# Two score banks more for the first four query blocks of a window-attention and MoE kernel

## The chip, the cores and the metric

The kernel runs as one program on one core of a Trainium2 chip. The metric is the device time of one execution in microseconds. The engines are TensorE (PE; its weight loads are PEld), VectorE (DVE), ScalarE (ACT), GpSimd (POOL) and SyncE (SP), which here only issues transfers. Each works through its own queue in order.

## What is computed

Window attention (batch 4, 8 heads, 576 positions, head size 64, a window of 64), a dense feed-forward layer of width 2048 with squared ReLU, and a top-1 mixture of 8 experts of width 1024, all in fp32:

```python
def reference(**kwargs):
    ...
    attn_out = _attn_ref(**attn_kwargs)          # softmax(mask(q k^T / 8)) v, 0 <= i - j < 64
    x = attn_out.transpose(0, 2, 1, 3).reshape(B * S, H * D)        # 2304 x 512
    x = _moe_ref(x=x, **moe_kwargs)              # h = max(x w_in, 0); (h * h) w_out
    return _moe2_ref(x=x, **moe2_kwargs)         # the best expert's max(x w1, 0) w2, times its gate
```

## The kernel before

The 2304 tokens go through attention and the dense layer in nine supertiles of 256 tokens. A supertile is four query blocks of 64 positions, all eight heads at once; block g of the first eight (two supertiles, NE = 8) is called g0 to g7 here. Behind them come g8 to g35, and at last the experts.

One block is a chain of eight stages (the tuple ATT): scores on PE (`att_scores`, L349: a mask matmul, then eight matmuls into one PSUM bank), the row maximum on DVE (L375) and its scaling on ACT (L378), four exps on ACT (L396), the division on GpSimd (L412), four transposes on PE (L418), a copy on ACT (L423), sixteen value matmuls on PE (L433), and a split of the result into a high part `xh` on ACT (L168) and a low part `xl` on DVE (L169). All matmuls of the dense layers take three products of such halves (L172 to L174).

PSUM has eight banks of 512 columns. The first eight blocks put their scores into two of them in turn, y0 and y1 (`ybanks[g % 2]`); y2 and y3 take the value products, a0 and a1 the transposes, h0 and h1 the hidden layer of the dense layer, which begins after the first four blocks.

Beside attention, the dense layer's weights are prepared, 16 chunks f0 to f15 of 128 hidden units. They arrive as 64-bit floats, 1 MB a chunk, two chunks deep in the buffers `stg`. A chunk takes an Abs on ACT (L189), four passes on DVE (L205, L206, L207, L210), two casts on ACT to the high half (L226) and two subtractions on GpSimd, some on DVE, to the low half (L228). The load of chunk f + 2 is issued when the passes of f are through (`conv_b`). Then the chunk's up-projection (`gemm1`) may run for a supertile, with ReLU (L462) and square (L469, L471, L478) behind it, and its down-projection (`gemm2`).

The order of the program is laid out by hand in slots, one for each pair of supertile and chunk. `chain(i, ATT, g, gaps)` (L893) puts a block's stages into slots from i on; the loop at L946 writes them out slot by slot, from slot -PRE on. Supertile 0 has slots 0 to 4 alone, then supertiles 1 and 0 alternate. A scheduler then reorders each engine's queue by its own estimate of the times, so a change of slots can also move instructions that it does not name.

Of the kernel before, what the change touches and what calls it, by code (L numbers as in the profile page):

```python
# [49 lines left out]
def kernel(  # L50
# [24 lines left out]
    QB = ST // W  # L75
# [79 lines left out]
    def psum(tag, bufs):  # L155
        return pr.tile([P, 512], F32, tag, bufs)

    ybanks = [pspool.tile([P, 512], F32, tag=f"y{i}", name=f"y{i}") for i in range(2 * TT)]
# [24 lines left out]
    def conv_a(f):  # L183
        i = (br.at["tmp"] + 1) % 4
        assert i % 2 == 0
        c = [br.tile([P, 512], I32, "tmp", 4) for _ in range(2)]
        whole = tmp2[i // 2].rearrange("p t n -> p (t n)")
        w = stg2[f % 2].bitcast(I32).rearrange("p t (n two) -> p (t n) two", two=2)
        nc.scalar.activation(whole.bitcast(F32), w[:, :, 1].bitcast(F32), ACTF.Abs)  # L189
        conv[f] = w[:, :, 0], w[:, :, 1], whole, c  # L190
# [109 lines left out]
    def load_q(g, n=1):  # L300
        b, i = divmod(g, NB)
        if g >= NE:
            qd[g] = br.tile([P, W, HP], F32, "qd", 1)
            nc.sync.dma_start(qd[g], qT[b, :, i])
            return
        qt = qfirst[:, g:g + n]
        for j in range(n):
            qk[g + j] = qfirst[:, g + j]
        if g > 1:
            for part in (qt[:D, :, W:], qt[D:, :, :W]):  # L310
                nc.scalar.copy(part, zero[:part.shape[0]].unsqueeze(2).unsqueeze(3).to_broadcast(part.shape))
        else:
            with tc.issue_after(made.ins):
                nc.vector.memset(qt[:D, :, W:], 0.0)
                nc.vector.memset(qt[D:, :, :W], 0.0)
        for half in range(2):
            rows = slice(half * D, half * D + D)
            nc.sync.dma_start(qt[rows, :, half * W:half * W + W, :], qT[b, rows, i:i + n])

    def lay_q(g):  # L320

        qk[g] = er.tile([P, HP, 2, W], F32, "q", 2)
        if g < NE + 2:
            with tc.issue_after(made.ins):
                nc.gpsimd.memset(qk[g][:D, :, 1, :], 0.0)
                nc.gpsimd.memset(qk[g][D:, :, 0, :], 0.0)
        d = qd.pop(g).rearrange("p s h -> p h s")
        for half in range(2):
            rows = slice(half * D, half * D + D)

            if g < NE + 5:
                nc.scalar.copy(qk[g][rows, :, half, :], d[rows])
            else:
                nc.gpsimd.tensor_copy(qk[g][rows, :, half, :], d[rows])  # L334
# [4 lines left out]
    def load_k(g, n=1):  # L339
        b, i = divmod(g, NB)  # L340
        nc.sync.dma_start(kfirst[:, g:g + n] if g < NB else kring[:, g % 4:g % 4 + n], kT[b, :, i:i + n])
# [7 lines left out]
    def att_scores(g):  # L349
        qt = qk.pop(g)  # L350
        k0 = g - 1 if g % NB else g
        if g < NE:
            ps = ybanks[g % 2]
            m = mask_b[:, 0 if g % NB else 1, :].unsqueeze(1).to_broadcast([P, HP, P])
            nc.tensor.matmul(ps.rearrange("p (h k) -> p h k", h=HP), lhsT=ident_b, rhs=m, start=True, stop=False)
        else:
            ps = psum("a", 2)
        for hp in range(HP):
            kt = kfirst[:, k0:k0 + 2] if g < NB else kring[:, k0 % 4:k0 % 4 + 2] if k0 % 4 < 3 else kring[:, 3::-3]
            nc.tensor.matmul(  # L360
                ps[:, hp * P:(hp + 1) * P], lhsT=qt[:, :, hp] if g < NE else qt[:, hp], rhs=kt[:, :, hp, :], start=g >= NE, stop=g >= NE or hp == HP - 1
            )
        if NE <= g < NS * QB - 1:
            lay_q(g + 1)
        if NE <= g < NS * QB - 2:
            load_q(g + 2)
        if NB < g < NS * QB - 3:
            load_k(g + 3)
        probs[g] = ps
# [510 lines left out]
    slot = {c: i for i, c in enumerate(order)}  # L880
    todo = {}
    ON_PE = (att_scores, att_transpose, att_values, gate_rank, early_pick, early_rows, early_tokens)

    def at(i, f, *args):
        todo.setdefault((i, f in ON_PE), []).append((f, args))

    def run(i, pe):
        for f, args in todo.pop((i, pe), ()):
            f(*args)
# [3 lines left out]
    def chain(i, stages, x, gaps, most=2):  # L893

        for f, gap in zip(stages, gaps):
            i += gap
            if f in ON_PE and i >= 0:
                while load.get(i, 0) >= most:
                    i += 1
                load[i] = load.get(i, 0) + 1  # L900
            at(i, f, x)
        return i

    ATT = (att_scores, att_max, att_exp, att_norm, att_transpose, att_evac, att_values, att_out)
    at(16, load_gates, 0)

# [2 lines left out]
            at(i + part, gate_dots, st, part)  # L909
        chain(i + E // 2, (gate_top, gate_rank, gate_slot), st, (0, 1, 1))  # L910

    PRE = 8
    for f in range(NF):
        i = max(-3, min(f - 1, slot[0, f] - 2))
        at(i, conv_c, f)
# [5 lines left out]
                  (0, load_k, 11), (0, load_k, 12), (0, load_wg, 0), (1, lay_q, NE), (1, load_q, NE + 1)):  # L921
        at(i, *l)
    for g in range(2 * QB):
        chain(g - PRE, ATT, g, (0, 1, 0, 1, 0, 1, 0, 1))
    for g in range(2 * QB, NS * QB):
        st, j = divmod(g, QB)
        i = slot[st, 0] - 19 + 4 * j
# [17 lines left out]
    conv_a(0)  # L945
    for i in range(-PRE, len(order) + LA):  # L946
        run(i, False)
# [207 lines left out]
```

## Time and profile before

| | |
|---|---|
| median of three runs | 835.53 us (834.1 to 836.63) |
| the profiled execution | 832.06 us, its span 829.9 us |
| PE busy | 787.3 us (95%) |
| DVE busy | 530.4 us (64%) |
| ACT busy | 398.8 us (48%) |
| POOL busy | 269.9 us (33%) |
| granted PE clock, mean | 0.987 of full speed |

The busy shares are means over stages with different limits: the opening, in which the first blocks and the dense layer's weights are prepared, the dense layer, and the experts behind it. The opening has to be read by stretches. A wait in these tables is idle time of an engine, with the instruction that ended it.

### The profile page before, as it was taken

To read this page: it belongs to the slowest core of one execution; us is meant where nothing else is said; L and a number is where in the kernel's file an instruction comes from. 1 tells how busy PE (TensorE), PEld (TensorE's weight loads), DVE (VectorE), ACT (ScalarE), POOL (GpSimd) and SP (SyncE) were. 2 spreads that over 40 slices of the span, in tenths; PEclk is the share of its full clock that TensorE was granted. 3 is DMA by queue.
4 is the path that set the end of the run, shared out by engine and by line. 5 is a ranking of instruction groups with operands and counts; after the bars stand their busy time and mean duration, and the time that the engine had idled before them with its cause. 6 is when DMAs were issued, how large, how long until landed. Compare 5 with 4: busy or idle time off the path is not lost.

```text
span 829.9 us, 14957 instructions
## 1 busy us (share of the span) xinstructions
PE 787.3 (95%) x5212; PEld 685.5 (83%) x5212; DVE 530.4 (64%) x1198; ACT 398.8 (48%) x1051; POOL 269.9 (33%) x262
## 2 busy tenths in 40 slices
PE   6889989999999999999999999989999999999894
PEld 5777878888888888888888897877898888888783
DVE  5799995984855947639467396568678654434110
ACT  6986663434444443534344345447577553434211
POOL 4646751112121221312211016165567541420201
PEclk9989999999999999999999999999999999999998
DMA  9845553111111111102020037366678644420101
GB/s 264 274 134 190 194 172 102 64 34 32 58 45 64 39 42 62 52 29 75 26 64 18 22 102 229 104 216 208 193 244 246 212 155 131 135 80 2 51 2 43
DMA packets 50860, 91.50 MB, mean 110 GB/s; under 512 B 8220, under 2 KB 24604, under 8 KB 50752
## 3 DMA queue, kind: packets, MB, share of 16 engines
q1 hardware_dynamic: 44688, 80.43, 30.3%
q0 software_dynamic: 6064, 9.63, 3.5%
q8 instruction: 69, 1.13, 0.6%
q14 instruction: 39, 0.32, 0.1%
HBM read 84.59 MB, written 13.81 MB: 119 GB/s over the span
## 4 chain that ended last, share of the span: by engine, by line
PE 66%; issue 13%; DVE 9%; DMA 5%; ACT 4%; POOL 1%; ACTq 0%; SPq 0%; POOLq 0%; DVEq 0%
PE h L172 11%; PE h L173 10%; PE h L174 10%; PE y L172 10%; PE y L174 9%; PE y L173 9%; PE a L360 2%; DMA stg<-in_moe_w_out 2%; PE a L433 2%; PE a L418 1%; DVE tmp L205 1%; DVE tmp L210 1%; PE a L683 1%; DVE tmp L207 1%; DMA out<-s,tab 1%
## 5 line engine op out<-in xcount | busy, mean ns | idle before, releaser
L172 PE MATMUL h<-xh,w 128*128 128x256 f32 (+3 forms) x864 | 262.9, 304 | 10.9 <-DVE gl L478 5.4
L174 PE MATMUL h<-xh,w 128*128 128x256 f32 (+3 forms) x864 | 255.6, 296 | 1.2 <-POOL w L228 1.2
L173 PE MATMUL h<-xl,w 128*128 128x256 f32 (+3 forms) x864 | 255.6, 296 | 0.9 <-DVE xl L169 0.5
L172 PEld LDWEIGHTS h<-xh,w 128*128 128x128 f32 x864 | 164.9, 191 | 27.6 <-DVE gl L478 9.6
L173 PEld LDWEIGHTS h<-xl,w 128*128 128x128 f32 x864 | 165.0, 191 | 9.1 <-DVE xl L169 0.9
L174 PEld LDWEIGHTS h<-xh,w 128*128 128x128 f32 x864 | 165.0, 191 | 4.3 <-POOL w L228 1.5
L462 ACT ACTIVATE r<-h 128x256 f32<-128x256 f32 x144 | 55.1, 382 | 203.7 <-PE h L174 197.9
L172 PE MATMUL y<-w,gh 128*128 128x512 f32 x294 | 119.2, 405 | 0.7 <-ACT gh L469 0.7
L770 DVE SCALAR_TENSOR_TENSOR ggl<-h,ggh 128x512 fp32r<-128x512 f32 (+1 forms) x69 | 46.2, 670 | 111.6 <-ACT ggh L769 111.5
L173 PE MATMUL y<-w,gh 128*128 128x512 f32 x294 | 116.4, 396 | 0.0
L471 DVE SCALAR_TENSOR_TENSOR h<-h,r 128x256 f32<-128x256 f32 x144 | 61.4, 426 | 84.0 <-ACT r L462 84.0
L174 PE MATMUL y<-w,gl 128*128 128x512 f32 x294 | 102.1, 395 | 0.5 <-DVE gl L770 0.5
L769 ACT ACTIVATE ggh<-h 128x512 fp32r<-128x512 f32 (+1 forms) x69 | 40.2, 583 | 125.5 <-PE h L174 96.2
L548 DVE SCALAR_TENSOR_TENSOR tmp<-tmp,stg 128x512 f32<-128x512 f32 x128 | 96.0, 750 | 0.8
L334 POOL COPY q<-qd 64x256 f32<-64x256 f32 x46 | 34.4, 749 | 143.9 <-PE a L360 142.5
L172 PE MATMUL y<-w,ggh 128*128 128x512 f32 x170 | 70.7, 416 | 0.0
L174 PE MATMUL y<-w,ggl 128*128 128x512 f32 x170 | 67.6, 398 | 1.7 <-DVE junk L996 1.1
L173 PE MATMUL y<-w,ggh 128*128 128x512 f32 x170 | 67.1, 395 | 0.0
L276 POOL TENSOR_TENSOR w<-stg,w 128x512 fp32r<-128x512 f32 x27 | 36.5, 1357 | 90.6 <-ACT w L275 87.6
L478 DVE TENSOR_TENSOR gl<-h,gh 128x256 fp32r<-128x256 f32 x144 | 60.5, 420 | 8.3 <-ACT gh L469 1.5
L172 PEld LDWEIGHTS y<-w,gh 128*128 128x128 f32 x294 | 55.6, 189 | 10.8 <-ACT gh L469 1.4
L173 PEld LDWEIGHTS y<-w,gh 128*128 128x128 f32 x294 | 55.6, 189 | 9.4
(165 smaller groups left out, 1262.4 us busy)
## 6 DMA issues: line engine op xcount, KB each, us to landing
stg<-in_moe_w SPq DMA_DIRECT2D x45, 512.0 KB, 4.0
stgx<-in_moe_w SPq DMA_DIRECT2D x18, 512.0 KB, 4.2
stg<-in_moe_w_in SPq DMA_DIRECT2D x16, 512.0 KB, 4.0
stg<-in_moe_w_out SPq DMA_DIRECT2D x16, 512.0 KB, 4.9
v<-in_v SPq DMA_DIRECT2D x28, 256.0 KB, 2.7
x_d<-tmp SPq DMA_DIRECT2D x18, 256.0 KB, 2.0
q<-in_moe_w SPq DMA_DIRECT2D x9, 512.0 KB, 4.5
qd<-in_q SPq DMA_DIRECT2D x28, 128.0 KB, 2.1
```

What stands on the lines that cost most here:

```text
L172: nc.tensor.matmul(o, lhsT=ah, rhs=bh, start=first, stop=False)
L173: nc.tensor.matmul(o, lhsT=ah, rhs=bl, start=False, stop=False)
L174: nc.tensor.matmul(o, lhsT=al, rhs=bh, start=False, stop=last)
L276: rest.tensor_tensor(l[:, a:a + 512], src, h[:, a:a + 512].bitcast(F32), op=ALU.subtract)
L334: nc.gpsimd.tensor_copy(qk[g][rows, :, half, :], d[rows])
L360: nc.tensor.matmul(ps[:, hp * P:(hp + 1) * P], lhsT=qt[:, :, hp] if g < NE else qt[:, hp], rhs=kt[:, :, hp, :], start=g >= NE, stop=g >= N ...
L462: nc.scalar.activation(r, gT[st, f][:, :ST], ACTF.Relu)
L471: nc.vector.scalar_tensor_tensor(out=ps[:, ST:2 * ST], in0=ps[:, :ST], scalar=0.0, in1=r, op0=ALU.max, op1=ALU.mult)
L478: nc.vector.tensor_tensor(gl, ps[:, ST:2 * ST], gh.bitcast(F32), op=ALU.subtract)
L548: nc.vector.scalar_tensor_tensor(out=junk, in0=x2sb[tt], scalar=1.0, in1=w, op0=ALU.mult, op1=ALU.mult, accum_out=l[:, t, e:e + 1])
L769: nc.scalar.activation(h[:, :width], hid[f][:, :width], ACTF.Relu)
L770: nc.vector.scalar_tensor_tensor(out=l[:, :width], in0=hid[f][:, :width], scalar=0.0, in1=h[:, :width].bitcast(F32), op0=ALU.max, op1=ALU. ...
```

## The change

The scores of g2 and g3 go into the banks h0 and h1 instead of y0 and y1. The chains of g0 to g3 start in pairs, at slots -6, -6, -5, -5 instead of -8, -7, -6, -5; those of g4 to g7 start at -3, -3, -2, -1 instead of -4, -3, -2, -1. The program begins at slot -6 instead of -8. The preparation of the weights keeps its slots.

```diff
--- before.py
+++ after.py
@@ -350,7 +350,8 @@
         qt = qk.pop(g)
         k0 = g - 1 if g % NB else g
         if g < NE:
-            ps = ybanks[g % 2]
+
+            ps = psum("h", 2) if g in (2, 3) else ybanks[g % 2]
             m = mask_b[:, 0 if g % NB else 1, :].unsqueeze(1).to_broadcast([P, HP, P])
             nc.tensor.matmul(ps.rearrange("p (h k) -> p h k", h=HP), lhsT=ident_b, rhs=m, start=True, stop=False)
         else:
@@ -909,7 +910,7 @@
             at(i + part, gate_dots, st, part)
         chain(i + E // 2, (gate_top, gate_rank, gate_slot), st, (0, 1, 1))
 
-    PRE = 8
+    PRE = 6
     for f in range(NF):
         i = max(-3, min(f - 1, slot[0, f] - 2))
         at(i, conv_c, f)
@@ -921,7 +922,8 @@
                   (0, load_k, 11), (0, load_k, 12), (0, load_wg, 0), (1, lay_q, NE), (1, load_q, NE + 1)):
         at(i, *l)
     for g in range(2 * QB):
-        chain(g - PRE, ATT, g, (0, 1, 0, 1, 0, 1, 0, 1))
+
+        chain(g // 2 - PRE if g < QB else max(-3, g - 2 * QB), ATT, g, (0, 1, 0, 1, 0, 1, 0, 1))
     for g in range(2 * QB, NS * QB):
         st, j = divmod(g, QB)
         i = slot[st, 0] - 19 + 4 * j
```

What this makes of the queues is shown at three places. A name like `y0_131` is a bank or buffer with its number in the program; `sf0` to `sf3` hold a block's exps; lines of the changed kernel are one higher from L354 on.

PE at the very start, before: `y0` and `y1` are the score banks, L355 is a block's mask matmul, L360 its scores.

```order
L355 MATMUL y0_131<-mask_b_139,ident_b_138 128x512
L355 LDWEIGHTS ident_b_138
L355 MATMUL y1_132<-mask_b_139,ident_b_138 128x512
L360 MATMUL y0_131<-kf_137,qf_135 128x128 x4
L360 MATMUL y1_132<-kf_137,qf_135 128x128 x4
L355 LDWEIGHTS ident_b_138
L355 MATMUL y0_131<-mask_b_139,ident_b_138 128x512
L360 MATMUL y0_131<-kf_137,qf_135 128x128 x4
L355 LDWEIGHTS ident_b_138
L355 MATMUL y1_132<-mask_b_139,ident_b_138 128x512
L360 MATMUL y1_132<-kf_137,qf_135 128x128 x4
L418 MATMUL a0_204<-ident_86,sf0_140 128x128 x4
```

With the change, the same place behind the four mask matmuls of g0 to g3:

```order
L361 MATMUL y0_131<-kf_137,qf_135 128x128 x4
L361 MATMUL y1_132<-kf_137,qf_135 128x128 x4
L361 MATMUL h0_201<-kf_137,qf_135 128x128 x4
L361 MATMUL h1_202<-kf_137,qf_135 128x128 x4
L356 LDWEIGHTS ident_b_138
L356 MATMUL y0_131<-mask_b_139,ident_b_138 128x512
L356 LDWEIGHTS ident_b_138
L356 MATMUL y1_132<-mask_b_139,ident_b_138 128x512
L419 MATMUL a0_231<-ident_86,sf0_140 128x128 x4
L361 MATMUL y0_131<-kf_137,qf_135 128x128 x4
L361 MATMUL y1_132<-kf_137,qf_135 128x128 x4
L419 MATMUL a1_232<-ident_86,sf1_141 128x128 x4
```

The scores of g2 and g3 stand ahead of everything else. The masks of g4 and g5 follow, and the scores of both now stand ahead of the second transpose (L419, `a1`), where one block's transposes stood between before.

ACT from the scaling of g2's maximum on, before: L396 are exps, L189 the Abs of chunk f1, L226 the casts of f0.

```order
L378 ACTIVATE nmax2_180<-nmax2_180 128x4
L396 ACTIVATE sf2_142,tot2_185<-y0_131,nmax2_180 128x128 x4
L189 ACTIVATE tmp1_77<-stg1_79 128x1024
L226 CAST w0_271<-tmp0_76 128x4x128
L226 CAST w1_272<-tmp0_76 128x512
L378 ACTIVATE nmax0_178<-nmax0_178 128x4
L423 COPY sf0_140<-a0_204 128x512
L423 COPY sf1_141<-a1_205 128x512
L396 ACTIVATE sf3_143,tot0_183<-y1_132,nmax0_178 128x128 x4
```

With the change:

```order
L379 ACTIVATE nmax2_185<-nmax2_185 128x4
L397 ACTIVATE sf2_142,tot2_190<-h0_201,nmax2_185 128x128 x4
L379 ACTIVATE nmax0_183<-nmax0_183 128x4
L189 ACTIVATE tmp1_77<-stg1_79 128x1024
L397 ACTIVATE sf3_143,tot0_188<-h1_202,nmax0_183 128x128 x4
L226 CAST w0_241<-tmp0_76 128x4x128
L226 CAST w1_242<-tmp0_76 128x512
L424 COPY sf0_140<-a0_231 128x512
L379 ACTIVATE nmax1_184<-nmax1_184 128x4
```

The exps of g3 (`sf3`) have moved from behind the casts and two copies to right behind the Abs of f1.

ACT some forty rows in, before: the exps of g7, the casts of f2 (from `tmp0`), the first ReLU (L462), the Abs of f3 (`tmp1`) and two copies of queries (L332).

```order
L396 ACTIVATE sf3_143,tot1_184<-y1_132,nmax1_179 128x128 x4
L226 CAST w0_271<-tmp0_76 128x4x128
L226 CAST w1_272<-tmp0_76 128x512
L462 ACTIVATE r0_460<-h0_434 128x256
L189 ACTIVATE tmp1_77<-stg1_79 128x1024
L332 COPY q_72<-qd0_411 64x4x64 x2
L469 ACTIVATE gh0_80<-r0_460 128x256
```

With the change:

```order
L397 ACTIVATE sf3_143,tot1_189<-y1_132,nmax1_184 128x128 x4
L463 ACTIVATE r0_454<-h0_201 128x256
L189 ACTIVATE tmp1_77<-stg1_79 128x1024
L332 COPY q_72<-qd0_404 64x4x64 x2
L226 CAST w0_241<-tmp0_76 128x4x128
L226 CAST w1_242<-tmp0_76 128x512
L463 ACTIVATE r1_455<-h1_202 128x256
L470 ACTIVATE gh0_80<-r0_454 128x256
```

The casts of f2 have moved behind the Abs of f3 and the copies, and the second ReLU ahead of the first square.

## Rows read from the trace of the kernel before

**Rows 1.** Stretches in us: PE, PEld, DVE, ACT, POOL busy (count), PEclk, DMA, GB/s

```profile
10.00:20.00 10.00, 6.98 (x32) 6.30 (x32) 7.69 (x15) 8.30 (x33) 3.38 (x3) 1.00 1.07 312
20.00:30.00 10.00, 9.05 (x86) 8.19 (x85) 8.19 (x14) 8.75 (x37) 7.36 (x6) 1.00 1.05 351
30.00:40.00 10.00, 8.32 (x91) 7.16 (x90) 7.58 (x16) 9.95 (x30) 5.33 (x6) 1.00 0.63 200
...
120.00:130.00 10.00, 9.19 (x56) 7.67 (x55) 10.00 (x14) 4.60 (x10) 2.96 (x2) 1.00 0.56 194
130.00:140.00 10.00, 10.00 (x64) 8.79 (x63) 4.54 (x11) 4.24 (x11) 2.54 (x2) 1.00 0.31 107
```

**Rows 2.** Waits of DVE, 8 to 45 us, then 45 to 132: total, times, longest

```profile
DVE nmax L375 <- PE y L360: 6.8, 5, 2.9
...
DVE tmp L205 <- ACT tmp L189: 3.3, 2, 2.7
...
DVE tot L410 <- ACT s L403: 0.6, 1, 0.6
```

**Rows 3.** ACT in order of time: start, duration, instruction [idle before <- who]

```profile
16.11 0.37 ACT L396 ACTIVATE sf<-y,nmax 128x128 f32<-128x128 f32 x1
...
17.49 1.13 ACT L189 ACTIVATE tmp<-stg 128x1024 f32<-128x1024 f32 x1
...
20.59 0.39 ACT L396 ACTIVATE sf<-y,nmax 128x128 f32<-128x128 f32 x1
...
29.60 1.13 ACT L189 ACTIVATE tmp<-stg 128x1024 f32<-128x1024 f32 x1
...
36.40 1.14 ACT L226 CAST w<-tmp 128x512 fp32r<-128x512 f32 x2
...
37.72 1.16 ACT L189 ACTIVATE tmp<-stg 128x1024 f32<-128x1024 f32 x1
```

**Rows 4.** PE in order of time, third score block

```profile
12.70 0.58 PE L355 MATMUL y<-mask_b,ident_b 128*128 128x512 bf16 x1 [3.25 <-ACT sf L396]
...
13.08 2.03 PE L360 MATMUL y<-kf,qf 128*128 128x128 f32 x8
```

**Rows 5.** Three loads as SyncE issues them, then each one's us to landing

```profile
5.17 0.59 SPq L341 DMA_DIRECT2D kf<-in_k  x1
...
7.37 0.74 SPq L234 DMA_DIRECT2D stg<-in_moe_w_out  x1
...
11.12 0.59 SPq L341 DMA_DIRECT2D kf<-in_k  x1
...
kf<-in_k SPq DMA_DIRECT2D x1, 256.0 KB, 6.2
...
stg<-in_moe_w_out SPq DMA_DIRECT2D x1, 512.0 KB, 9.2
...
kf<-in_k SPq DMA_DIRECT2D x1, 256.0 KB, 7.2
```

**Rows 6.** DVE in order of time, maxima and weight passes

```profile
15.14 0.69 DVE L375 TENSOR_REDUCE nmax<-y 128x4 f32<-128x512 f32 x1 [0.86 <-PE y L360]
...
19.38 1.41 DVE L206 TENSOR_SCALAR tmp<-tmp 128x1024 int32<-128x1024 int32 x1
...
37.57 0.97 DVE L228 TENSOR_TENSOR w<-tmp,w 128x512 fp32r<-128x512 f32 x1 [0.52 <-ACT w L226]
...
40.13 1.64 DVE L206 TENSOR_SCALAR tmp<-tmp 128x1024 int32<-128x1024 int32 x1
...
44.76 1.21 DVE L210 SCALAR_TENSOR_TENSOR tmp<-stg,tmp 128x1024 int32<-128x1024 int32 x1
```

**Rows 7.** Line L206, the second pass: ns min/median/max of 16

```profile
L206 DVE TENSOR_SCALAR tmp<-tmp x16: 674/1018/1693, 12.3 to 125.4; 128x1024 int32<-128x1024 int32 x16
```

**Rows 8.** Waits of PE, 35 to 160 us

```profile
PE h L174 <- POOL w L228: 1.2, 1, 1.2
```

**Rows 9.** A stretch, columns as in the first group

```profile
56.00:58.00 2.00, 1.86 (x8) 1.87 (x9) 2.00 (x2) 2.00 (x11) 1.32 (x2) 0.50 0.22 76
```


## The prediction

> **What bounds the kernel now.** I read the page first. TensorE (PE) is busy 95% of the span, so the time can only come from the few places where PE stands still, and the change touches the first 130 us alone. The slices of the page show VectorE (DVE) nearly full there and thinning out behind; the table by stretch [rows 1] says it exactly: DVE is busy 10.00 of 10 us from 120 to 130 us and 4.54 from 130 to 140, while PE goes from 9.19 to 10.00. So until the last weight chunk is converted, near 130 us, DVE sets the pace; behind that PE does, without a gap. DVE converts 16 weight chunks f0 to f15 by four passes each, beside attention and the squares. What shortens the kernel is therefore DVE having less idle or stretched time before 130 us, not PE starting sooner. From 45 us on its longest wait is 0.6 us [rows 2], while between 10 and 40 us it idles 2.3, 1.8 and 2.4 us in each ten [rows 1]: the idle time to be had lies there.
>
> There the waits of DVE [rows 2] name two things: 6.8 us for scores on PE and 3.3 us for the Abs pass (L189) on ScalarE (ACT). ACT is the engine both hang on: it is busy 8.30 of 10 us from 10 to 20 and 9.95 from 30 to 40 [rows 1]. The queue of ACT in order of time [rows 3] shows why: the exps of block g2 begin at 16.11, g3's at 20.59, and only then the rest follows. g2's scores waited 3.25 us for ACT to empty g0's bank [rows 4].
>
> **The change, part by part.** I name the eight first query blocks g0 to g7. All clock readings for the new kernel are worked out here by going down the new order of each engine with the durations of the rows.
>
> 1. Banks h for g2 and g3. Four mask matmuls instead of two come before the first scores; one took 0.58 [rows 4], and they lie beside the wait for the first queries, so they cost nothing (1.2 us at most, hidden by ACT, which waits for f0's weights longer than that). g2's scores no longer wait for g0's exps but for their keys: issued at 5.17, landed 6.2 us later, 11.4 [rows 5]. Eight matmuls take 2.03 [rows 4], so 13.4; the maximum takes 0.69 [rows 6], the scaling 0.3, and ACT is free by then. The exps of g2 begin at 14.45, not 16.11 [rows 3]: 1.7 us sooner.
>
> 2. g3 now comes behind f1's Abs in ACT's order, and that needs f1's weights: issued at 7.37 and 9.2 us on the way [rows 5], so 16.6. Abs takes 1.03 until the next instruction can start, and a block of exps 1.38 (16.11 to 17.49, [rows 3]), so g3's begin at 17.6 and end at 19.0; before they began at 20.59: 3.0 sooner. This is the gain that the change can show locally.
>
> 3. Most of it is given back at once. g4's keys are issued at 11.12 and land 7.2 us later, 18.3 [rows 5], which the change does not touch. Its scores end at 20.3, and the new order puts g5's scores (2.0) before the second transpose (0.6) on PE. So ACT, after the casts of f0 (19.0 to 20.0) and one copy (0.5), has only a small scaling to do until 22.8: 2.2 of the 3.0 us are idle. From there to f2's Abs it has the same instructions as before, and that Abs starts at 28.65, not 29.60 [rows 3]: 0.95 sooner. Its weights, now behind one more 256 KB of values on the SyncE queue, land near 28.4, so nothing more is to be had there.
>
> 4. f3's Abs starts at 36.05, not 37.72: 1.67 sooner. But 1.03 of that is borrowed: the two casts of f2 stood ahead of it at 36.40 [rows 3] and now stand behind it and two copies, at 38.4. Net 0.65.
>
> 5. DVE. f3's four passes now start at 37.1. With undisturbed durations (0.66, 0.67, 1.13 and 1.13 from start to start, one subtraction of 0.97 as in [rows 6] and three short instructions of 0.33 between them) its last pass ends at 42.7, not 45.9 [rows 6]. The kernel before had by then also done f4's first pass (0.60), so DVE leads by 2.6. That is the upper end. In the kernel before, however, passes were stretched: f1's second took 1.41 and f3's second 1.64 [rows 6], against a minimum of 0.674, and the median of 16 is 1.018 [rows 7]. That is 0.73 and 0.96, and with 0.27 on f1's third pass 1.96 that my walk did not charge. GpSimd works beside them as before (its norms of g2 and g7 fall on f1's and f3's second passes), so if all of it returns the lead is 0.6: the lower end of what the order alone gives. I take 1.2, nearer to the lower end because the GpSimd work is the same in number and the same kinds overlap.
>
> On those stretches the Trainium skill (SBUF — State Buffer, "Who interferes with whom") says that VectorE and GpSimd hold a shared port pair exclusively for a whole instruction. The spread 0.674 to 1.693 of one shape agrees [rows 7]. By that rule alone the new order would keep the stretches where GpSimd's norms fall, which is the lower end, 0.6.
>
> 6. Blocks g4 to g7 move by at most one slot, and everything from g8 on keeps its slot; the scheduler only swaps neighbours there. I cost this at 0, with 1 us either way as its bound, about one stretched pass [rows 7]; DVE's full queue hides it.
>
> The sum: the profiled execution took 832.06 (span 829.9 and 2.2 around it). Minus 1.2 is 830.9. The median of the three runs shown is 835.53, 3.5 above the profiled one, so against the median the forecast is 834.3. A change below 0.3%, 2.5 us, cannot be told from none.
>
> **The rivals.**
>
> Faster: the stretches do not return, since f1's and f3's passes fall into gaps of GpSimd, and the same happens at some later chunks. For it: 16 chunks have them, and the second pass has a median 0.34 above its minimum [rows 7], 5 us over all chunks. Against it: the GpSimd work is unchanged. The lead is 2.6, or 3.5 with a few later passes: 832.0 to 832.9.
>
> No change: ACT's lead of 0.65 is eaten by DVE's new waits. Going down the new order, DVE waits for g0's cast near 25 (1.6 us), for g6's scores (1.0), for f2's Abs (0.75) and for g7's scores (1.3); in all some 6 us from 11 to 40, and before it was about as much, 6.5 [rows 1]. Then 835.5.
>
> Slower: f2's two casts come 2.0 us later (step 4), and in the new order the exps of g8 and g9 stand ahead of f4's casts. PE gets its third and fifth weight chunk late. PE waited 1.2 us for GpSimd's part of such a chunk in the kernel before [rows 8], and ran at a granted clock of 0.50, 1.2 GHz, from 56 to 58 us [rows 9]. If these waits grow by 2.0 at f2 and 1.5 (one exp block) at f4 and PE, not DVE, carries the time, the end comes 3.5 later: 839.0. It decides from the point where PE has more queued work than DVE, that is where DVE begins to wait for PE between 40 and 130 us. Against it: in that stretch DVE has no wait for PE of any size [rows 2]. On the clock the Trainium skill (TensorE: Matmul & The Clock Gate, "HAM oscillation — how this bites in real kernels") says that waits between bursts send it back to half; the row agrees, and a second such stretch would be part of this rival's price.
>
> **How the numbers follow.** Forecast 0.40, faster rival 0.25, no change 0.17, slower rival 0.18. Faster by more than 0.3% (below 833.0): most of the faster rival and the forecast's tail, 0.28. Slower by more than 0.3% (over 838.0): most of the slower rival and a little of the rest, 0.18. Within: 0.54. The range runs from the faster rival's middle less the runs' own spread of some 1.5 us, 830.8, to the slower rival, 839.0; the likeliest case alone has 833.1 to 835.5.
>
> **What would show it.** g2's exps near 14.5, g3's near 17.6, and an idle ACT between about 20.5 and 22.8: steps 1 to 3. f2's Abs near 28.7 and f3's near 36: step 4. The first up-projection matmul 0.5 to 1.5 us sooner than before, but the first down-projection hardly sooner. DVE full from 40 us to about 129. If DVE's share falls between 40 and 130, or PE waits there for casts longer than before, the slower rival is right. If the four passes have lower means than before, the faster one is. I am wrong in principle if the last weight pass moves by one amount and the end by another.

## The result and the profile after

The changed kernel is slower: 840.76 us (median of five runs, 840.11 to 842.71) against 835.53 for the kernel before (five runs beside them), a ratio of 1.0084 (95% interval 1.0063 to 1.0104), some 7 us (5.3 to 8.7 by the interval; the two medians alone differ by 5.2). The profiled execution took 840.76 us with a span of 838.7, 8.8 longer than before's. The forecast, 1.2 us faster, and its range up to 839.0 both missed; a loss of more than 0.3% had been given a chance of 0.18.

The opening first: the table by stretch of the changed kernel, with the columns of [rows 1].

```profile
10.00:20.00 10.00, 6.68 (x28) 5.75 (x28) 8.36 (x15) 8.95 (x39) 3.73 (x3) 0.82 1.07 328
20.00:30.00 10.00, 7.80 (x64) 6.88 (x64) 7.97 (x11) 6.57 (x24) 9.59 (x7) 0.84 1.01 341
30.00:40.00 10.00, 9.39 (x111) 8.55 (x111) 8.28 (x17) 9.94 (x35) 2.73 (x4) 1.00 0.34 113
120.00:130.00 10.00, 7.71 (x38) 6.67 (x38) 9.80 (x12) 5.26 (x11) 5.27 (x4) 0.83 0.55 176
130.00:140.00 10.00, 10.00 (x69) 9.18 (x68) 5.71 (x11) 3.60 (x9) 2.55 (x2) 1.00 0.44 140
```

Against [rows 1], PE does less from 10 to 30 us and, far behind the opening, 1.5 us less from 120 to 130. GpSimd is nearly full from 20 to 30. ACT's queue, to be read against [rows 3], in order of time:

```profile
14.43 0.37 ACT L397 ACTIVATE sf<-h,nmax 128x128 f32<-128x128 f32 x1
16.49 1.13 ACT L189 ACTIVATE tmp<-stg 128x1024 f32<-128x1024 f32 x1 [0.23 <-DMA stg<-in_moe_w_out]
18.22 0.37 ACT L397 ACTIVATE sf<-h,nmax 128x128 f32<-128x128 f32 x1 [0.60 <-POOL sf L413]
24.16 0.20 ACT L379 ACTIVATE nmax<-nmax 128x4 f32<-128x4 f32 x1 [2.92 <-DVE nmax L376]
30.73 1.23 ACT L189 ACTIVATE tmp<-stg 128x1024 f32<-128x1024 f32 x1
38.26 1.22 ACT L189 ACTIVATE tmp<-stg 128x1024 f32<-128x1024 f32 x1
40.68 1.14 ACT L226 CAST w<-tmp 128x512 fp32r<-128x512 f32 x2
```

The exps of g2 begin at 14.43 and g3's at 18.22, both sooner than before. Then ACT stands idle for 2.92 us, and the Abs of f2 and f3 come at 30.73 and 38.26: 1.1 and 0.5 us *later* than in [rows 3]. GpSimd's queue shows one reason:

```profile
16.27 4.36 POOL L413 TENSOR_TENSOR sf<-sf,tot 128x512 f32<-128x512 f32 x3 [9.46 <-ACT nmax L379]
20.60 4.00 POOL L228 TENSOR_TENSOR w<-tmp,w 128x512 fp32r<-128x512 f32 x2
24.55 2.02 POOL L413 TENSOR_TENSOR sf<-sf,tot 128x512 f32<-128x512 f32 x1
```

Three divisions run in one row from 16.27 to 20.6. Before, the same three stood apart and began earlier:

```profile
14.45 1.03 POOL L412 TENSOR_TENSOR sf<-sf,tot 128x512 f32<-128x512 f32 x1 [7.64 <-DVE tot L411]
17.27 1.04 POOL L412 TENSOR_TENSOR sf<-sf,tot 128x512 f32<-128x512 f32 x1 [1.79 <-DVE tot L411]
18.69 1.55 POOL L412 TENSOR_TENSOR sf<-sf,tot 128x512 f32<-128x512 f32 x1 [0.38 <-ACT tmp L189]
```

The reciprocal that the first division needs (L412 of the changed kernel) stands behind the maxima of g2 and g3 in DVE's queue; g3's is the row above it:

```profile
15.33 0.69 DVE L376 TENSOR_REDUCE nmax<-h 128x4 f32<-128x512 f32 x1
15.94 0.17 DVE L412 RECIPROCAL tot<-tot 128x4 f32<-128x4 f32 x1
```

What this makes of the whole is best read at one instruction: the copy on DVE of supertile 0's output (L496, L497 after), which waits for that supertile's last matmul. Before, with the last pass (L210) of the last weight chunk f15 above it:

```profile
129.42 1.21 DVE L210 SCALAR_TENSOR_TENSOR tmp<-stg,tmp 128x1024 int32<-128x1024 int32 x1
145.14 0.69 DVE L496 COPY tmp<-y 128x512 f32<-128x512 f32 x1 [2.53 <-PE y L174]
```

and after:

```profile
132.46 1.21 DVE L210 SCALAR_TENSOR_TENSOR tmp<-stg,tmp 128x1024 int32<-128x1024 int32 x1
152.33 0.69 DVE L497 COPY tmp<-y 128x512 f32<-128x512 f32 x1 [2.53 <-PE y L174]
```

The last weight pass comes 3.0 us later, the output copy 7.2 us. From there on the two executions run side by side: the same copy of each of the next seven supertiles comes 7.2 us later too, that of the ninth 6.7. The rest of the 8.8 us in span arises among the experts, behind 526 us, and does not seem to come from the change: E9 below, with the order of before, has the first eight of these copies 0.2 us sooner than before and yet a span 2.1 us longer. PE's account up to that copy, before (PE busy is the second number of a row, idle what is left to the first):

```profile
0.00:27.00 27.00, 18.11 (x118) 15.74 (x118) 17.52 (x34) 19.69 (x66) 13.45 (x31) 1.00 0.95 288
27.00:55.00 28.00, 23.78 (x208) 20.17 (x207) 23.99 (x40) 23.61 (x61) 13.76 (x11) 0.99 0.59 193
55.00:100.00 45.00, 41.85 (x303) 36.29 (x304) 43.67 (x69) 33.43 (x92) 28.54 (x20) 0.93 0.54 181
100.00:145.14 45.14, 42.21 (x272) 35.72 (x271) 35.40 (x53) 22.27 (x52) 18.29 (x13) 1.00 0.41 139
```

and after:

```profile
0.00:27.00 27.00, 18.14 (x101) 15.13 (x102) 17.77 (x30) 17.62 (x56) 16.44 (x32) 0.87 0.95 305
27.00:55.00 28.00, 24.11 (x223) 20.63 (x221) 24.90 (x43) 25.58 (x77) 10.45 (x9) 1.00 0.47 149
55.00:100.00 45.00, 38.73 (x275) 32.16 (x275) 44.93 (x64) 30.40 (x78) 28.25 (x19) 0.96 0.54 179
100.00:152.33 52.33, 46.92 (x301) 41.36 (x302) 39.14 (x59) 25.19 (x62) 20.45 (x14) 0.97 0.41 136
```

PE's idle time is 8.9, 4.2, 3.2 and 2.9 us before, 8.9, 3.9, 6.3 and 5.4 after. PE loses nothing up to 55 us; 3.1 us are lost from 55 to 100 and 2.5 behind that, in all 5.2. PE's busy time grows by 1.9; the rows do not say by what. Two of the waits:

```profile
57.43 0.58 PE L172 MATMUL h<-xh,w 128*128 128x256 f32 x1 [2.98 <-ACT w L226]
...
125.45 0.42 PE L172 MATMUL h<-xh,w 128*128 128x256 f32 x1 [2.29 <-DVE gl L479]
```

The first is mostly not new: before, PE waited for `w`, a chunk's weights, at that place twice, 1.1 and 1.2 us. What has grown most is the wait for the subtraction on DVE that makes `gl`, the low part of a chunk's square: it is the last to read a bank `h`, into which a later up-projection goes. Waits of PE up to 150 us (total, times, longest), two lines of the changed kernel behind three of before:

```profile
PE h L172 <- DVE gl L478: 3.7, 7, 1.1
PE h L174 <- POOL w L228: 1.2, 1, 1.2
PE h L172 <- ACT w L226: 1.1, 1, 1.1
...
PE h L172 <- DVE gl L479: 7.1, 8, 2.3
PE h L172 <- ACT w L226: 3.0, 1, 3.0
```

So 3.4 of the 5.2 us are waits for `gl`, that is for a free bank `h`, and 0.7 are waits for weights. Behind each of the two waits stands a stretch at a granted clock of 0.50 (1.2 GHz), near 58 to 60 and 126 to 128 us. Before had only one such stretch, at the first place [rows 9], but a longer one; its next row and the changed kernel's second stretch:

```profile
58.00:60.00 2.00, 2.00 (x7) 1.71 (x7) 2.00 (x6) 2.00 (x7) 0.00 (x0) 0.50 0.04 8
...
126.00:128.00 2.00, 2.00 (x11) 2.00 (x11) 1.87 (x4) 1.80 (x3) 0.04 (x1) 0.50 0.18 55
```

By the mean clocks in PE's account (0.93 and 1.00 against 0.96 and 0.97) both kernels spend about as long at half clock behind 55 us, so the clock does not explain the loss there. (The clock falls in the changed opening, too: 0.82 and 0.84 in the rows further up. PE idles no more there for it.) The question for the experiments is why an edit to the first four blocks makes PE wait a hundred microseconds later.

### The profile page after: what moved, and what is told of

It is laid out like the page before. It is cut to its first block, busy times and chain, and to the rows that moved or that the text cites. A ratio compares the mean times of both kernels' runs of the same rounds, so it can differ in the third digit from the quotient of the medians.

```text
span 838.7 us, 14952 instructions
## 1 busy us (share of the span) xinstructions
PE 790.4 (94%) x5212; PEld 687.5 (82%) x5212; DVE 536.0 (64%) x1198; ACT 398.3 (47%) x1051; POOL 271.1 (32%) x262
## 4 chain that ended last, share of the span: by engine, by line
PE 66%; issue 14%; DVE 11%; DMA 4%; ACT 2%; POOL 1%; SPq 0%; POOLq 0%; DVEq 0%; ACTq 0%
PE h L172 11%; PE h L173 10%; PE h L174 10%; PE y L172 10%; PE y L174 10%; PE y L173 9%; PE a L361 2%; DVE tmp L207 2%; PE a L434 2%; DVE w L276 1%; DVE tmp L210 1%; PE a L419 1%; PE a L684 1%; DVE tmp L205 1%; DMA stg<-in_moe_w_out 1%
```

## The experiments

Every run is compared with runs of the kernel before on the same chip. In all of them I read the same copy of supertile 0's output. The last column is 834 us times the ratio less 1.

| kernel | f15's last pass ends | output copy | shift | ratio (95%) | in us |
|---|---|---|---|---|---|
| before | 130.6 | 145.14 | | 1 | |
| changed | 133.7 | 152.33 | +7.2 | 1.0084 (1.0063 to 1.0104) | +7.0 |
| E1 banks alone | 136.2 | 153.55 | +8.4 | 1.0089 (1.0063 to 1.0116) | +7.4 |
| E2 slots alone | 130.9 | 145.39 | +0.3 | 1.0014 (0.9994 to 1.0033) | +1.2 |
| E3 changed, 22 low parts | 136.5 | 150.95 | +5.8 | 1.0071 (1.0046 to 1.0097) | +5.9 |
| E4 before, 21 low parts | 134.3 | 151.60 | +6.5 | 1.0081 (1.0055 to 1.0107) | +6.8 |
| E5 changed, reciprocals first | 132.7 | 147.30 | +2.2 | 1.0044 (1.0030 to 1.0058) | +3.7 |
| E6 changed, transposes first | 133.9 | 148.51 | +3.4 | 1.0056 (1.0042 to 1.0070) | +4.7 |
| E7 changed, no additions | 136.7 | 154.35 | +9.2 | 1.0112 (1.0097 to 1.0128) | +9.3 |
| E8 before, no additions | 132.6 | 148.43 | +3.3 | 1.0041 (1.0028 to 1.0055) | +3.4 |
| E9 banks, queues of before | 130.5 | 144.97 | -0.2 | 0.9991 (0.9971 to 1.0010) | -0.8 |
| E10 banks, opening free | 132.3 | 146.85 | +1.7 | 1.0025 (1.0006 to 1.0045) | +2.1 |
| E11 before, 23 low parts | 132.2 | 145.23 | +0.1 | 0.9996 (0.9978 to 1.0013) | -0.3 |
| E12 banks, queues of E11 | 132.0 | 145.07 | -0.1 | 0.9985 (0.9963 to 1.0007) | -1.3 |
| E13 banks, own queues, no additions | 133.2 | 151.11 | +6.0 | 1.0057 (1.0042 to 1.0073) | +4.8 |
| E14 before, own queues, no additions | 130.0 | 144.48 | -0.7 | 0.9968 (0.9955 to 0.9981) | -2.7 |

Shift and measured time agree within 2 us in every row: the place of the loss is found. E1, which has the changed kernel's queues, differs from it by 1.2 us in shift, so smaller differences between two rows of this column say little. The reason took more.

Two theories stood at the start. A: the opening loses the time, since GpSimd's divisions bunch there and stretch DVE's instructions, and the last weight pass comes 3.0 us later. B: the order behind the opening leaves PE one chunk of 2.8 us more behind the last weight pass.

**E1 and E2: which half of the change.** The banks alone are the first hunk of the diff, the slots alone the other two.

```diff
-            ps = ybanks[g % 2]
+            ps = psum("h", 2) if g in (2, 3) else ybanks[g % 2]
```

> Only the two score banks, the slots as in the kernel before. Its queues come out in exactly the order of the changed kernel on every engine. If the order is all that counts, it takes the changed kernel's time, 840.8 within 1.5 us (ratio to before 1.006 to 1.010), and the slots are without effect. If the slots mattered by themselves, it would be anywhere else.

> Only the new slots and the shorter start, the score banks as before. Its queues come out in exactly the order of the kernel before. Order theory: 835.5, ratio 0.998 to 1.002. If starting two slots sooner had an effect of its own, faster by 1 to 3 us.

The banks alone lose all of it, the slots alone nothing that can be told. The order of the instructions says why: with the banks alone every engine's queue stands as in the changed kernel, and with the slots alone as in the kernel before. The scheduler undoes the move of the slots. (The 1.2 us of E2 are then no effect, but a measure of how far off such a comparison can be.)

**E3 and E4: one chunk more behind the last weight pass.** In DVE's queue the low part of a chunk's square (`gl`) stands 22 times ahead of f15's last pass before, 21 times after. A chunk takes PE 2.81 us where nothing holds it up. An edge of order alone, with no wait on it, sets this balance:

```diff
+        d = nc.vector.tensor_tensor(gl, ...)
+        n = marks["n"] = marks.get("n", 0) + 1
+        for last, least in enumerate((0, 0, 0, 2, 3, 4, 5, 7, 9, 11, 13, 15, 16, 18, 20, 22)):
+            if least == n:
+                behind(marks["last", last], d)
```

E4 does the opposite in the kernel before (at most 0, 0, 0, 1, 3, ... 21).

> The changed kernel with one thing added: VectorE's order of weight passes and chunk products behind the opening is held as in the kernel before (22 instead of 21 chunks' low parts ahead of the last weight pass). Theory A (the opening loses the time: VectorE stretched by GpSimd, its last weight pass 3.0 us later): stays at 838 to 841. Theory B (the order behind the opening leaves PE one chunk of 2.8 us more to do when the weights are through): falls by about 2.8 to 4, to 837 to 838, with VectorE's last weight pass unchanged near 133.6.

> The kernel before with the opposite thing: each low part beyond the changed kernel's count is held behind the weight pass (21 instead of 22 ahead of the last one), the opening as before. Theory A: 835.5, no change. Theory B: slower by about 2.8, 838.3, with the last weight pass near 130 to 131.

E3 took the distance from the last pass to the copy back to 14.5 us, but its last pass came at 136.5, and nothing was won that stands clear of the noise (1.0071 against 1.0084). E4 lost 6.5 us where one chunk is worth 2.8, and its last weight pass came at 134.3 instead of 130 to 131. So it is not the count. But E4 moves only queue positions behind the opening, no work, and costs as much as the change: order alone can do it. In E4, too, the largest wait of PE is that for `gl`, 7.8 us where before has 3.7:

```profile
PE h L172 <- DVE gl L478: 7.8, 10, 1.8
```

**E5 and E6: two places of the opening.** E5 holds the reciprocals of g0 and g1 ahead of the maxima of g2 and g3, E6 the scores of g5 behind g1's transposes, by the same kind of edge.

```diff
+            behind(marks['max', g + 2], marks['recip', g])   # E5, g = 0, 1
+                behind(d, marks['turned'])                   # E6, scores of g5
```

> The changed kernel with the reciprocals of g0 and g1 held ahead of the maxima of g2 and g3 on VectorE, so that GpSimd divides g0's scores near 14.5 as in the kernel before and not at 16.3, and the divisions stand apart; the second transpose then comes ahead of g4's scores by itself. Theory A: the stretched small VectorE instructions (L411 of the changed kernel, 0.45 us in the mean) go back to 0.2, g4's maximum comes 2 us sooner, f2's Abs near 29 instead of 30.7, and the time falls to 835 to 837. Theory B: only as far as the order behind it changes too (22 chunks ahead of the last pass here): 837 to 838.

> The changed kernel with g5's scores held behind the transposes of g1 on PE, nothing else held; VectorE's opening stays as in the changed kernel up to g4's maximum. If PE's order there is the loss, f2's Abs comes about 2 us sooner and the time is 836 to 838. If the loss is that g4's maximum waits on VectorE behind stretched passes (near 23.5), f2's Abs stays near 30.5; the time then falls only by the order behind it (22 chunks ahead of the last pass), to 837 to 838.

Both win something back (some 3 and 2 us, each known to some 2 us), but not as forecast: both stay above their ranges (by 3.7 and 4.7 us over before, some 839 and 840 on the expectations' scale), and f2's Abs, which was to come near 29 in E5 and 2 us sooner or unchanged in E6, came at 30.44 and 32.03. Neither says which part of the gain is the opening: with each edge the scheduler plans the queues behind the opening anew too.

**E7 and E8: less work for DVE.** The addition of 1e-9 to the softmax sums is left out, 36 instructions of 128x4, with nothing else changed.

```diff
-        nc.vector.tensor_scalar_add(tot, tot, 1.0e-9)
```

> The changed kernel without the addition of 1e-9 to the row sums (36 small VectorE instructions, each a collision partner of GpSimd). Theory A: these took 6.3 us for 14 in the opening against 3.0 in the kernel before; without them the changed kernel gains 4 to 6 us, 835 to 837, more than the kernel before gains by the same edit (2 to 3). Theory B: it gains its order's 2.8 (22 chunks ahead) and the plain length of the instructions, 836 to 838.

> The kernel before without the addition of 1e-9 to the row sums: the control for the run before. Theory A: VectorE is rid of 3.0 us in the opening, so 833 to 834. If VectorE's length before 130 us does not set the end, 835.5.

Both kernels became *slower* by taking work away: the changed one from 1.0084 to 1.0112 (just clear of the noise), the one before from 1 to 1.0041. A theory of DVE's load cannot explain this; all forecasts of the two runs failed. In both the queues had been planned anew. So the order itself had to be held.

**E9 and E10: the banks without the new order.** The banks alone, with the instructions of the first 130 us and more on PE, DVE, ACT and GpSimd chained by such edges in the order in which the built kernel before has them. The loads are left free (the expectation of E9 speaks of five engines; the edges hold these four): they come as before in E9 and as in the changed kernel in E10. E9 holds all of them, E10 only those behind the opening, from the first up-projection (some 27 us) on.

```diff
+    for rows in QUEUES.values():
+        queue = ...
+        for a, b in zip(queue, queue[1:]):
+            tc.add_manual_dep(nc.get_inst_by_name(b), a, NOSYNC, reason='order')
```

> The change's banks (blocks 2 and 3 in the two h banks), with every queue of the five engines up to some 300 us held in the order of the kernel before. Order theory (the banks cost nothing, all that is lost is lost by the order in which the queues then stand): ratio 1.000 +- 0.002, last pass of the last weight chunk (L210) near 130.6 us, the copy of the first supertile's output near 145.1 us. If the earlier scores help once the order is kept, up to 1.5 us less. Rival, the banks themselves cost (block 2's and 3's scores in the h banks hold up the first GEMM, or earlier exps run into the weight passes): the 6 to 7 us stay, ratio 1.006 to 1.009.

> The change's banks with the order that they bring in the opening (to the first GEMM, some 27 us) left as it is, and every queue behind it held in the order of the kernel before, so that no chunk's low part moves behind the last weight pass. Two-part theory: the opening's share stays (last L210 1.5 to 3 us later than before's 130.6) and the chunk's share (2.8 us and the wait beside it) goes: ratio 1.002 to 1.004, the output copy 14.5 us behind the last L210. Rival, all lies in the order behind the opening: 1.000. Rival, all lies in the opening: 1.007 to 1.009.

These two show where the loss lies. With the old queues the banks cost nothing, 0.9991 (0.9971 to 1.0010). The opening as the change brings it, with the old order behind it, costs 1.0025 (1.0006 to 1.0045), so some 2 us of the 7 (0.5 to 3.8); the other 5 (known to some 2.4) are the order behind the opening. This takes the two parts as a sum; the fourth combination, the old opening with the changed order behind it, was not run. PE's account of E10, to be read like the two above:

```profile
0.00:27.00 27.00, 18.64 (x114) 15.98 (x114) 17.82 (x30) 17.71 (x56) 14.06 (x30) 0.75 0.95 285
27.00:55.00 28.00, 24.76 (x212) 21.92 (x208) 23.48 (x43) 24.02 (x69) 12.86 (x10) 0.94 0.52 171
55.00:100.00 45.00, 39.91 (x295) 34.15 (x295) 43.65 (x70) 34.17 (x93) 28.08 (x19) 0.96 0.54 184
100.00:146.85 46.85, 43.98 (x284) 37.26 (x283) 37.12 (x56) 23.43 (x55) 20.14 (x14) 1.00 0.43 146
```

Behind 100 us PE idles 2.9 us, as before, where the changed kernel has 5.4; from 55 to 100 it idles 5.1, where before has 3.2 and the changed kernel 6.3. Up to the copy its idle time is 4.9 us less than the changed kernel's, and 3.8 of these are again waits for `gl`, which stand as low as before:

```profile
PE h L172 <- DVE gl L478: 3.3, 6, 1.1
```

In the opening, GpSimd's queue in E9:

```profile
13.99 1.03 POOL L412 TENSOR_TENSOR sf<-sf,tot 128x512 f32<-128x512 f32 x1 [7.15 <-DVE tot L411]
16.41 1.04 POOL L412 TENSOR_TENSOR sf<-sf,tot 128x512 f32<-128x512 f32 x1 [1.39 <-DVE tot L411]
17.83 1.35 POOL L412 TENSOR_TENSOR sf<-sf,tot 128x512 f32<-128x512 f32 x1 [0.38 <-DVE tot L411]
```

and in E10:

```profile
16.58 4.36 POOL L412 TENSOR_TENSOR sf<-sf,tot 128x512 f32<-128x512 f32 x3 [9.75 <-ACT nmax L378]
```

The divisions start 2.6 us later and in one row when the reciprocals stand behind the maxima; f2's last pass ends at 38.1 instead of 35.6. Before it ended at 36.4, and this lag of 1.7 us is still there, at 1.7, in E10's last pass of f15 and in its output copy. In E9, where the new banks could help, that pass comes 0.8 us sooner than before (35.6 against 36.4), and of this lead 0.2 is left at f5 and 0.1 at f15.

**E11 and E12: a version with one chunk more ahead.** If the tail counts in chunks, 23 low parts ahead of f15's last pass should gain. E11 puts E3's edges into the kernel before, with another list; E12 has the banks with E11's queues.

```diff
-        ... 13, 15, 16, 18, 20, 22
+        ... 13, 15, 17, 19, 21, 23
```

> The kernel before, with one chunk's square and low part (L471, L478) more ahead of the last weight passes in VectorE's queue: 23 low parts ahead of the last L210 instead of 22. Chunk theory: the last L210 comes 0.75 us later (131.4), one chunk of 2.81 us less is left behind it, output copy 11.7 us behind the last L210, in all 2 us less: ratio 0.9975, 831.5 to 833 where before has 833.5 to 835. Rival, TensorE has no room for the chunk ahead of the last pass (it idles 2.9 us between 100 and 130 us): no change, 1.000.

> The change's banks with all queues held in the order of the kernel of the run before this one (before's order with one chunk more ahead of the last weight pass). Order theory: as that run, ratio 0.9975, or up to 1.5 us less if block 2's earlier scores help. Banks theory: 1.004 to 1.006.

```profile
131.00 1.22 DVE L210 SCALAR_TENSOR_TENSOR tmp<-stg,tmp 128x1024 int32<-128x1024 int32 x1
145.23 0.69 DVE L500 COPY tmp<-y 128x512 f32<-128x512 f32 x1 [2.53 <-PE y L174]
```

In E11 the last pass moves by 1.6 us and the copy not at all: the rival was right, PE has no room there. The chunk theory falls a second time. E12 is level with before, too.

**E13 and E14: the additions again, the order held.** The additions are left out as in E7 and E8, but every other instruction of the first supertile is held where it stood: in the order that the banks bring (E13), in before's (E14).

> The change's banks without the addition of 1e-9 to the softmax sums (36 VectorE instructions of 128x4; this part of the computation is left out), with every other instruction of the first supertile held in the order that the banks bring. Collision theory (part of the loss is VectorE's time in these small additions, 6.3 us for 14 of them where before's took 3.0): the last L210 comes 3 us sooner than in the banks alone and the end with it, ratio 1.004 to 1.006 where the banks alone had 1.0089. Order theory (TensorE's idle time comes from where the squares and casts stand, and VectorE's time only shifts into waits): less than 1.5 us gained, 1.007 to 1.009.

> The kernel before without the same 36 additions (this part of the computation is left out), with every other instruction of the first supertile held in before's order. Order theory: the loss of the earlier run without the additions (1.0041) came from the queues being planned anew; with the order held it is gone, 0.997 to 1.000, the last L210 0 to 3 us sooner than 130.6. Rival, the small additions pace something that is good for the kernel: 1.003 to 1.005 again.

Now both are faster: 1.0089 to 1.0057 and 1 to 0.9968, 0.0032 each, where the first difference is known only to 0.003. So the additions cost some 2.7 us in the kernel before, and the gap of 0.0089 between the two orders stays. E13 taken alone came out as the collision theory said (1.004 to 1.006, and the last L210 3.0 us sooner than in E1), not as the order theory said; it is the equal gain of E14 that speaks against collisions. The shifts are less equal: without the additions the copy comes 2.4 us sooner than in E1, but only 0.7 sooner than in before. What bounds the stretched additions better is E10: its 14 additions take as long as the changed kernel's (6.0 and 6.3 us, where before has 3.0), and its whole loss is 2.1 us. So they are not what most of the change's loss is made of; whether they have a part in these 2 us is not shown. E14 is the one version that beats both kernels clear of the noise. The addition can go: every sum holds the exp of its own maximum, near 1, and in fp32 1e-9 is rounded away beside it.

## Why the prediction was wrong

**Steps 1 and 2** held in the main. g2's exps began at 14.43 (14.45 was forecast), g3's at 18.22 (17.6; ACT waited 0.60 for a division). The mask matmuls cost nothing: the first scores began at 5.5 us (5.4 before), and ACT's first exps where they did before.

**Step 3** had the idle time of ACT right in kind (2.92 us instead of 2.2), but not what follows: f2's Abs came at 30.73, not 28.65. The walk took GpSimd's divisions where they stood before, but their reciprocals had moved behind two maxima, so that they came later and in one row.

**Step 4** gave f3's Abs 36.05 and f2's casts 38.4; they came at 38.26 and 40.68, both more than 2 us later, handed on from step 3.

**Step 5**, the term of -1.2 us, had the wrong sign: E10, which has this opening and before's order behind it, is 2.1 us slower (0.5 to 3.8).

**Step 6** is the step that failed most. Its words are "the scheduler only swaps neighbours there. I cost this at 0, with 1 us either way as its bound"; it measured 5 us (changed kernel less E10). They are not only neighbours, either: up to 160 us instructions stand up to 9 places from where they stood on DVE, and up to 17 on ACT. The reason given, that DVE's full queue hides it, does not hold, since DVE's own order sets when the subtraction for `gl` frees a bank `h`: PE's waits for it are 7.1 us in the changed kernel, 3.3 in E10.

**The frame** behind the sum, DVE full to 130 us and therefore the bound, was half right. With the order held, work taken from DVE does shorten the kernel (E14, and less surely E13). But I then reckoned only in DVE's time, and most of the loss is PE's: 5.2 us more idle time up to the first output. The prediction's own sign of being wrong in principle came true: the last weight pass moved by 3.0 us, the end by 7. The slower rival came near in size (839.0), but mostly by luck: it named the late casts, where PE waits 2.98 us at 57.43 but had waited 1.1 and 1.2 at that place before, and a second stretch at half clock, which did come but adds no time at half clock in all; it did not name the waits for `gl`. It was given 0.18, because in the kernel before DVE waits for nothing of PE there; that row is of the old order and could say nothing of the new. That the slots do nothing (E2) was not foreseen, and could have been read from the program.

What stays open: which of the swaps behind the opening costs how much. E3 to E8 show that each of these six new plannings of the queues loses 3 to 9 us against the order that the kernel before has, but not by what rule. In the opening, that the late reciprocals are the reason for the 2 us is read from E9 and E10 side by side, and not tried alone with the rest held. The two differ in more: E10's PE runs at a granted clock of 0.75 up to 27 us (E9's at 0.94), and one load of values is issued earlier.

## What to carry to other kernels

Where a scheduler sets the queues, an edit is two edits: the one that is meant and the new order of everything beside it. Build both programs, and where the queues differ far from the edit, give that difference a range of its own as wide as such reorderings have cost, not 0. To test a mechanism, hold the order by edges that add no wait (E9, E14) and change one thing: without that, E7 and E8 would have taught that removing work makes a kernel slower.

## What the runs showed of the hardware

A tiny instruction can be held by a neighbour for longer than its own work. The additions and reciprocals of 128x4 in the changed kernel, up to 130 us (count, then min, median and max in ns):

```profile
L411 DVE TENSOR_SCALAR tot<-tot x14: 137/159/1234, 14.1 to 114.1; 128x4 f32<-128x4 f32 x14
L412 DVE RECIPROCAL tot<-tot x14: 161/168/179, 15.9 to 115.1; 128x4 f32<-128x4 f32 x14
```

Same shape, same place in the program, and only the addition is stretched. Five of the 14 additions run beside an instruction of GpSimd: these five take 0.78 to 1.23 us, and each ends some 0.03 us behind the end of one. The other nine take 0.14 to 0.16. Five of the reciprocals run beside one, too, and take no longer than the rest. One of the five additions:

```profile
17.30 0.92 DVE L411 TENSOR_SCALAR tot<-tot 128x4 f32<-128x4 f32 x1
```

It ends at 18.22, just behind GpSimd's division, which ends at 18.19, and ACT's exps of g3, which waited for that division, begin then. By the Trainium skill (SBUF — State Buffer, "Summary: rules for kernel authors") an instruction of VectorE in a 2-port mode that is issued second is blocked until GpSimd's has finished. The additions' rows agree, though no run shows in which mode they work; the reciprocals' show that not every instruction of VectorE is held.
